# A unit's addition of sums tied behind a bank that VectorE empties, in a kernel of windowed attention and a gated feed-forward

## The chip, the cores and the metric

The kernel runs on one core of one Trainium2 chip. The metric is the device time of one execution in microseconds. Engines: TensorE (PE, with its weight loads PEld), VectorE (DVE), ScalarE (ACT), GpSimd (POOL) and SyncE (SP), which here issues nearly all transfers. Each engine takes its instructions in order.

## The reference

`x` has 2048 tokens of 512 values. It is normalised, goes through attention with 32 heads of 16 over a window of 256 tokens, and through a gated feed-forward of width 1792; the one output is gated by the other.

```
xn = layernorm(x)
q, k, v = split(xn @ wqkv)                        # 32 heads of 16
scores = where(0 <= i - j < 256, q k^T / 4, -1e9)
s = (softmax(scores) @ v) @ wo
h = silu(xn @ w1) * (xn @ w3)
out = x + s * silu(h @ w2)
```

## The kernel before

Products are made of float16 halves, a high and a low part, three matmuls for one. The tokens are cut into four tiles of 512 (`t`), the heads into four groups of eight (`g`); a tile and group are worked on in two **units** (`p`), each of four heads, 32 units in all. I count units from 0.

For a unit the kernel first finds the largest score of every row (`pass1`: scores by L619 into a PSUM bank, the maximum by L633 on VectorE), two units ahead, and then makes the scores again transposed (`pass2`: scores by L695, masks added by L702 on VectorE, the exponential by L705 on ScalarE) and multiplies them with the values (L723) into the PSUM tile `po`. There are two banks for scores (`s`); a bank is free when its maximum or its exponential has been taken. `po` has two halves, for the two halves of the keys, and a row of every head holds the sum of the exponentials.

When a unit's last chunk is multiplied, `finish` copies the first half to `os` on ScalarE (L733), and two steps later `rest` adds the second half on VectorE (L739). Then come the transfers: four of `os` into `on` (L745) and one of the sums into `dd` (L746). After the second unit of a tile and group `normalise` loads the sums as `dr` (L761); `invert` takes the reciprocal on VectorE (L765, L766), stores it as `de` (L768), spreads it by eight loads into `rb` (L772) and multiplies `on` by it on GpSimd (through `halves`, L307); `cut` makes the two float16 halves of the result (L778 on ScalarE, L307 on GpSimd), which the output projection reads (L996, `total`).

Attention alone would not fill TensorE. So each unit is run as five **batches** of scores (`batches`), and between them stands a share of dense work (`spread`): gate and up projections (`gate_up`, L897), the down projection (`down`, L946), the projections of q, k and v (L563, L533) and the output projection. A dense product goes into one of two PSUM banks `m0` and `m1` in turn (`bank`), and the bank must be emptied before TensorE comes to it again: on VectorE by L576 (q and k), L916 and L921 (gate and up), L967 and L970 (down) and L1000 (output), partly with an earlier copy on ScalarE (L572, L912).

Two things set the order. TensorE's instructions stand in the order in which the program makes them; those of the other engines are placed by a scheduler from their order in the program, their priority and its estimate of when their inputs are there. `urgent()` raises the priority. `tc.issue_after(ins)` makes the instructions in its block stand behind `ins` on the same engine, without a wait for a semaphore. And `later(n, f)` runs `f` after n more **steps**, where a step is one batch or one dense piece, some 18 of them in a unit; so it says how far on in the program the instructions of `f` are made.

Of the kernel before, what the change touches and what calls it, by code (L numbers as in the profile page):

```python
# [79 lines left out]
def tile_block(ctx: ExitStack, tc: tile.TileContext, x, wqkv, wo, w1, w3, w2, out):  # L80
# [466 lines left out]
    def project(t, g, k, terms=(range(3),), scores_bank=False):  # L547


        cell = {}  # L550

        parts = ([[(c, i) for c in (2 * half, 2 * half + 1) for i in range(3)] for half in range(2)] if len(terms) == 1
                 else [[(c, i) for i in group for c in range(NC)] for group in terms])

        def part(n):
            assert turned[t] == 4
            hi, lo, _ = WQK[g]
            xh, xl = X[t]
            if n == 0:
                cell["pp"] = pss.tile([P, 2, TW], F32, name="s")[:, 0, :] if scores_bank else bank([P, TW])  # L560
            for c, i in parts[n]:
                a, b = ((hi, xh), (lo, xh), (hi, xl))[i]
                nc.tensor.matmul(cell["pp"], a[:, k, c, :], b[:, c, :], start=(c, i) == parts[0][0],  # L563
                                 stop=(c, i) == parts[-1][-1])
            if n < len(parts) - 1:
                return
            pp = cell["pp"]
            both = take(F16)
            B = both.rearrange("p (a t) -> p a t", a=2)
            s = QS / (XS * WS)  # L570
            with urgent():
                nc.scalar.activation(B[:, 0, :], pp, AF.Copy, scale=s)  # L572

            def rest():
                with urgent():
                    nc.vector.scalar_tensor_tensor(B[:, 1, :], pp, s, B[:, 0, :], op0=ALU.mult, op1=ALU.subtract)  # L576
                d = (dQ, dK)[k][g][:, :, t * TW:(t + 1) * TW]
                if k == 0:
                    nc.sync.dma_start(d[:, 0:2, :], B[:, 0:1, :].to_broadcast([P, 2, TW]))
                    nc.sync.dma_start(d[:, 2, :], B[:, 1, :])  # L580
                else:
                    nc.sync.dma_start(d[:, 0:2, :], B)
                    nc.sync.dma_start(d[:, 2, :], B[:, 0, :])
                give(both, after=4)
            later(1, rest)
        return opening([(len(l), lambda n=n: part(n)) for n, l in enumerate(parts)])

# [86 lines left out]
    def pass2(t, g, p):  # L674

        es = WQK[g][2]
        cell = {}
        chunks = CHUNKS if t else FIRST

        def pieces(c):  # L680

            which, *halves, _ = chunks[c]
            for n in range(max(map(len, halves))):
                for a in which:
                    for h in range(2):
                        for piece in halves[h][n:n + 1]:
                            yield 256 * a * (len(which) - 1) + 64 * piece[3], h, a, piece

        def scores(c):
            qa, ka = QA[t, g], keys(t, g)  # L690
            s = scores_bank()
            for o, h, a, (m, k, n, _, _) in pieces(c):
                for r in range(2):
                    rows = slice(64 * r, 64 * r + KR + 2)
                    nc.tensor.matmul(s[64 * h:64 * h + 64, r, o:o + 64 * n], ka[rows, 2 * p + a, 64 * (m + 4):64 * (m + 5)],  # L695
                                     qa[rows, 2 * p + a, 64 * (m + k):64 * (m + k + n)], start=True, stop=True)
            which, *_, masks = chunks[c]
            sv = s.rearrange("p r (a k q) -> p (r a) k q", a=len(which), q=64)
            for first, by, n, kind, of in masks:
                v = sv[:, :, first:first + by * (n - 1) + 1:by, :]  # L700
                with urgent():
                    nc.vector.tensor_add(v, v, MK[:, kind, of:of + n, :].unsqueeze(1).to_broadcast([P, 2 * len(which), n, 64]))  # L702
            cell[c] = pt = ppool.tile([P, 2, 512], F32, name="pt")
            with urgent():
                nc.scalar.activation(pt, s, AF.Exp, scale=es)  # L705

        begun = set()

        def values(*cs):

            if not begun:
                cell["po"] = pso.tile([P, 2, TW], F32, name="po")
            turns = {}
            for c in cs:
                for item in pieces(c):
                    if item[3][4]:
                        turns.setdefault(item[1:3], []).append((c, *item))
            for group in zip_longest(*(turns[k] for k in sorted(turns))):
                for c, o, h, a, (m, k, n, _, _) in filter(None, group):
                    for r in range(2):  # L720
                        i = 2 * r + a
                        hd = g * 8 + r * 4 + 2 * p + a
                        nc.tensor.matmul(cell["po"][32 * i:32 * i + 32, h, 64 * (m + k):64 * (m + k + n)],  # L723
                                         V[64 * h:64 * h + 64, (4 * t + m // 2) % VB, hd * VW:hd * VW + 32],
                                         cell[c][64 * h:64 * h + 64, r, o:o + 64 * n],
                                         start=(h, i) not in begun, stop=c == len(chunks) - 1, skip_group_check=True)
                        begun.add((h, i))

        def finish():
            os = opool.tile([P, TW], F32, name="os", bufs=1)  # L730
            po = cell["po"]
            with urgent():
                nc.scalar.copy(os, po[:, 0, :])  # L733

            def rest():

                c = slice(0 if t else 64, TW)
                with urgent():
                    nc.vector.tensor_add(os[:, c], os[:, c], po[:, 1, c])  # L739
                if p == 0:  # L740
                    ON[t, g] = (opool.tile([P, TW], F32, name="on", bufs=1), dpool.tile([8, TW], F32, name="dd"))
                on, dd = ON[t, g]
                for i in range(4):
                    h = (i // 2) * 4 + 2 * p + i % 2
                    nc.sync.dma_start(on[16 * h:16 * h + 16, :], os[32 * i:32 * i + 16, :])  # L745
                nc.sync.dma_start(dd[4 * p:4 * p + 4, :], os[DH::32, :])  # L746
                if p == 1:
                    normalise(t, g)

            later(2, rest)  # L750

        def last(*cs):
            values(*cs)
            finish()
        n = len(chunks)
        return [lambda c=c: scores(c) for c in range(n)], lambda *cs: (last if cs[-1] == n - 1 else values)(*cs)

    def normalise(t, g):
# [16 lines left out]
        def cut():  # L775
# [1 line left out]
            O[t, g] = o = made.rearrange("p (a q) -> p a q", a=2)  # L777
            nc.scalar.copy(o[:, 0, :], on)  # L778
            halves(nc.gpsimd.tensor_sub, o[:, 1, :], on, o[:, 0, :])
        later(8, invert)  # L780
        later(24, cut)

# [101 lines left out]
    def gate_up(t, f):  # L886
        cell = {}

        def part(k, half):
# [18 lines left out]
            if k == 0:  # L908
                cell["s"] = sg = take(F32)

                with urgent():
                    nc.scalar.activation(sg, cell[0], AF.Tanh, scale=sg_scale[:, f:f + 1])  # L912

                def product():
                    with urgent():
                        nc.vector.scalar_tensor_tensor(sg, sg, 1.0, cell[0], op0=ALU.add, op1=ALU.mult)  # L916
                later(1, product)
            else:
                sg = cell["s"]
                with urgent():  # L920
                    nc.vector.scalar_tensor_tensor(sg, cell[1], 0.5 * HS / (WS * XS)**2, sg, op0=ALU.mult, op1=ALU.mult)  # L921
                HH[t, f] = hh = take(F16)

                def rest():
                    nc.scalar.copy(hh[:, 0:TW], sg)  # L925
                    halves(nc.gpsimd.tensor_sub, hh[:, TW:], sg, hh[:, 0:TW])
                    give(sg, after=4)
                later(1, rest)
# [5 lines left out]
    def down(t, k, b):  # L934
# [4 lines left out]
        def part(fs):  # L939
# [21 lines left out]
            if k == 0:  # L961
                ACC[t, b] = take(F32)
                with urgent():
                    if t:
                        nc.scalar.activation(ACC[t, b], ps, AF.Copy, scale=down_scale[:, 0:1])
                    else:
                        nc.vector.tensor_scalar(ACC[t, b], ps, down_scale[:, 0:1], None, op0=ALU.mult)  # L967
            else:
                with urgent():
                    nc.vector.scalar_tensor_tensor(ACC[t, b], ps, down_scale[:, k:k + 1], ACC[t, b], op0=ALU.mult, op1=ALU.add)  # L970
        return opening([(3 * len(fs), lambda fs=fs: part(fs)) for fs in (range(f0, f0 + 2), range(f0 + 2, f1))])

    def residual(t, b):
# [3 lines left out]
    def total(t, b):  # L977
# [4 lines left out]
        def part(half):  # L982
# [14 lines left out]
                                     stop=g == NG - 1 and i == 2)  # L997
            if half:
                with urgent():
                    nc.vector.scalar_tensor_tensor(y, ps, sc["y"], y, op0=ALU.mult, op1=ALU.mult)  # L1000
                if t == NT - 1:
                    nc.vector.tensor_add(y, y, XR[t, b])
                else:
# [326 lines left out]
```

## Time and profile before

| | |
|---|---|
| time, median of 3 runs | 830.6 us (830.26 to 831.95) |
| the profiled execution | 831.77 us, its span 830.0 us |
| TensorE busy | 806.0 us, 97% of the span |
| VectorE busy | 609.4 us, 73% |
| ScalarE, GpSimd busy | 406.0 us, 205.9 us |
| transfers | 110.65 MB, 133 GB/s on average |
| mean granted TensorE clock | 0.996 |

How to read it: a line of the profile that begins with a time is an instruction, or several equal ones in a row, on the engine's time line: start, duration, engine, source line, operation, what it writes and reads, shapes. In brackets behind it stands how long the engine was idle before it and whose end released it. In the list of waits, `DVE os L739 <- ACT os L733: 30.4, 24, 4.6` reads: VectorE stood 30.4 us before L739, in 24 waits of which the longest was 4.6 us, until L733 on ScalarE had ended.

### The profile page before, as it was taken

The page shows a single profiled execution, that of the slowest core. Times are in us where ns is not written, and L with a number is a line of the kernel's source. Part 1 is how long each engine was busy: PE and PEld are TensorE (multiplying, and loading weights), DVE is VectorE, ACT ScalarE, POOL GpSimd, SP SyncE. Part 2 cuts the span into 40 slices and gives each one's busy share as a digit, 9 for nine tenths or more (in the row PEclk, how much of TensorE's full clock was granted, in tenths as well). Part 3 has the DMA queues.
Part 4 walks back from the last instruction along what each step waited for, and adds up shares of the span by engine and source line. Part 5 has one row for each costly group of instructions (what it writes and reads, how often), then busy time and mean ns, then how long its engine had stood idle before and what let it go on. Part 6 is the DMA issues. An engine that isn't in the chain of part 4 may idle for free. (4 is left out here: it accounts for less than half of the span.)

```text
span 830.0 us, 22908 instructions
## 1 busy us (share of the span) xinstructions
PE 806.0 (97%) x8924; PEld 381.5 (46%) x8924; DVE 609.4 (73%) x1989; ACT 406.0 (49%) x594; POOL 205.9 (25%) x355
## 2 busy tenths in 40 slices
PE   8999889999999999999999999999999999999998
PEld 4434335544445444444444544444444444444444
DVE  8787687877697668778878777777677787676435
ACT  6889686644536444344343444443443444443521
POOL 2238174242213203121211211121111113030211
PEclk9999989999999999999999999999999999999999
DMA  9978556166533354544543444544545253343211
GB/s 282 268 231 236 183 158 208 58 172 196 151 104 101 98 146 124 158 119 135 145 108 88 103 112 133 135 110 117 136 105 142 80 140 95 102 127 89 66 20 53
DMA packets 95324, 110.65 MB, mean 133 GB/s; under 512 B 17200, under 2 KB 60528, under 8 KB 95216
## 3 DMA queue, kind: packets, MB, share of 16 engines
q1 hardware_dynamic: 94928, 108.67, 46.9%
q8 instruction: 70, 1.15, 0.6%
q10 hardware_dynamic: 288, 0.52, 0.2%
q14 instruction: 38, 0.31, 0.1%
HBM read 76.28 MB, written 28.57 MB: 126 GB/s over the span
## 5 line engine op out<-in xcount | busy, mean ns | idle before, releaser
L307 POOL TENSOR_TENSOR slot<-slot,slot 128x256 f16<-128x256 f32 (+1 forms) x228 | 151.4, 691 | 528.0 <-ACT slot L925 416.1
L897 PE MATMUL m<-XH,slot 128*128 128x512 f16 x896 | 268.2, 381 | 10.5 <-DVE slot L967 3.6
L705 ACT ACTIVATE pt<-s,es 128x1024 f32<-128x1024 f32 x152 | 167.5, 1113 | 171.6 <-DVE s L702 168.4
L897 PEld LDWEIGHTS <-slot 128*128 128x128 f16 x1344 | 125.2, 98 | 166.7 <-issue 23.0
L897 PE MATMUL m<-XL,slot 128*128 128x512 f16 x448 | 170.3, 380 | 0.0
L946 PE MATMUL m<-slot,slot 128*128 128x512 f16 x672 | 156.3, 380 | 1.1 <-DVE slot L576 0.7
L702 DVE TENSOR_TENSOR s<-s,MK 128x256 f32<-128x256 f32 (+2 forms) x280 | 118.4, 435 | 49.5 <-PE s L695 48.5
L633 DVE CUSTOM_DVE_ANT_0 junk<-s,MW 128x320 bf16<-128x320 f32 x276 | 134.3, 486 | 24.9 <-PE s L619 16.0
L946 PEld LDWEIGHTS <-slot 128*128 128x128 f16 x672 | 61.8, 98 | 79.2 <-issue 8.5
L633 DVE CUSTOM_DVE_ANT_0 junk<-po,MW 128x320 bf16<-128x320 f32 x172 | 83.6, 486 | 5.1 <-DVE al L279 0.4
L723 PE MATMUL po<-pt,V 64*32 64x320 f32 (+4 forms) x2880 | 77.2, 342 | 0.1
L925 ACT CAST slot<-slot 128x512 f16<-128x512 f32 x56 | 34.5, 616 | 69.9 <-DVE slot L921 69.6
L723 PEld LDWEIGHTS po<-pt,V 64*32 64x32 f32 x2880 | 51.1, 106 | 21.6 <-issue 0.8
L695 PE MATMUL s<-qa,KA 50*64 50x320 f16 (+3 forms) x1472 | 58.3, 260 | 0.7 <-ACT pt L705 0.7
L916 DVE SCALAR_TENSOR_TENSOR slot<-slot,m 128x512 f32<-128x512 f32 x56 | 38.3, 685 | 27.8 <-ACT slot L912 27.6
L695 PEld LDWEIGHTS <-KA 50*64 50x64 f16 x1472 | 30.4, 106 | 55.0 <-issue 37.0
L912 ACT ACTIVATE slot<-m,sgs 128x512 f32<-128x512 f32 x56 | 38.3, 684 | 30.7 <-PE m L897 30.4
L619 PE MATMUL s<-KA,qa 48*64 48x320 f16 (+3 forms) x824 | 45.6, 295 | 3.3 <-ACT pt L705 2.4
L921 DVE SCALAR_TENSOR_TENSOR slot<-m,slot 128x512 f32<-128x512 f32 x56 | 38.5, 687 | 12.0 <-PE m L897 11.4
L970 DVE SCALAR_TENSOR_TENSOR slot<-m,dsc,slot 128x512 f32<-128x512 f32 x48 | 35.9, 748 | 14.2 <-PE m L946 13.9
L563 PE MATMUL m<-XH,whi 128*128 128x512 f16 x120 | 45.2, 385 | 0.4 <-DVE slot L921 0.4
L739 DVE TENSOR_TENSOR os<-os,po 128x512 f32<-128x512 f32 (+1 forms) x32 | 21.5, 671 | 32.2 <-ACT os L733 30.4
(162 smaller groups left out, 892.7 us busy)
## 6 DMA issues: line engine op xcount, KB each, us to landing
slot<-dW SPq DMA_DIRECT2D x126, 256.0 KB
slot<-in_B_w_dram SPq DMA_DIRECT2D x42, 256.0 KB
dW<-slot SPq DMA_DIRECT2D x42, 256.0 KB
slot<-in_A_x_dram SPq DMA_DIRECT2D x30, 256.0 KB
KA<-dK SPq DMA_DIRECT2D x24, 288.0 KB
qa<-dQ SPq DMA_DIRECT2D x32, 192.0 KB
dQ<-slot SPq DMA_DIRECT2D x16, 256.0 KB
dK<-slot SPq DMA_DIRECT2D x16, 256.0 KB
```

Of the source, the lines that this page charges most:

```text
L307: op(out[:, c], a[:, c], b[:, c])
L563: nc.tensor.matmul(cell["pp"], a[:, k, c, :], b[:, c, :], start=(c, i) == parts[0][0], stop=(c, i) == parts[-1][-1])
L619: nc.tensor.matmul(s[c:c + w, r, :n], qa[rows, 2 * p + a, ii * P + c:ii * P + c + w], ka[rows, 2 * p + a, e - n:e], start=True, stop=True)
L633: lasts["maximum"] = nc.vector.tensor_tensor_reduce(out=junk[:, :n], in0=s[:, r, :n], in1=mask, scale=1.0, scalar=NEG, op0=ALU.add, op1=AL ...
L695: nc.tensor.matmul(s[64 * h:64 * h + 64, r, o:o + 64 * n], ka[rows, 2 * p + a, 64 * (m + 4):64 * (m + 5)], qa[rows, 2 * p + a, 64 * (m + k ...
L702: nc.vector.tensor_add(v, v, MK[:, kind, of:of + n, :].unsqueeze(1).to_broadcast([P, 2 * len(which), n, 64]))
L705: nc.scalar.activation(pt, s, AF.Exp, scale=es)
L723: nc.tensor.matmul(cell["po"][32 * i:32 * i + 32, h, 64 * (m + k):64 * (m + k + n)], V[64 * h:64 * h + 64, (4 * t + m // 2) % VB, hd * VW: ...
L897: nc.tensor.matmul(cell[k], w[:, (a * NC + c) * P:(a * NC + c + 1) * P], b[:, c, :], start=c == 0 and i == 0, stop=c == NC - 1 and i == 2)
L912: nc.scalar.activation(sg, cell[0], AF.Tanh, scale=sg_scale[:, f:f + 1])
L921: nc.vector.scalar_tensor_tensor(sg, cell[1], 0.5 * HS / (WS * XS)**2, sg, op0=ALU.mult, op1=ALU.mult)
L946: nc.tensor.matmul(ps, hh[:, a * TW + b * P:a * TW + (b + 1) * P], w[:, c * D:(c + 1) * D], start=f == f0 and i == 0, stop=f == f1 - 1 and ...
```

## The change

Each instruction with which VectorE empties a dense bank is noted in `lasts["emptied"]`, six places in all. The addition L739 is placed behind the last one noted, on VectorE. The transfers that follow it are a function of their own, `send`, run two steps after the addition. `invert` is due nine instead of eight steps after `normalise`, so three steps later in all; `cut` 22 instead of 24, so at the same step as before. No instruction is added or taken away.

```diff
             def rest():
 
                 c = slice(0 if t else 64, TW)
-                with urgent():
+
+                with urgent(), tc.issue_after(lasts["emptied"].ins):
                     nc.vector.tensor_add(os[:, c], os[:, c], po[:, 1, c])
+                later(2, send)
+
+            def send():
                 if p == 0:
                     ON[t, g] = (opool.tile([P, TW], F32, name="on", bufs=1), dpool.tile([8, TW], F32, name="dd"))
...
-        later(8, invert)
-        later(24, cut)
+        later(9, invert)
+        later(22, cut)
...
                 def product():
                     with urgent():
-                        nc.vector.scalar_tensor_tensor(sg, sg, 1.0, cell[0], op0=ALU.add, op1=ALU.mult)
+                        lasts["emptied"] = nc.vector.scalar_tensor_tensor(sg, sg, 1.0, cell[0], op0=ALU.add, op1=ALU.mult)
...
                 with urgent():
-                    nc.vector.scalar_tensor_tensor(ACC[t, b], ps, down_scale[:, k:k + 1], ACC[t, b], op0=ALU.mult, op1=ALU.add)
+                    lasts["emptied"] = nc.vector.scalar_tensor_tensor(ACC[t, b], ps, down_scale[:, k:k + 1], ACC[t, b],
+                                                                      op0=ALU.mult, op1=ALU.add)
```

The two shown are L916 and L970; L576, L921, L967 and L1000 are noted in the same form.

More of the change, by code (lines that the diff above doesn't have):

```diff
@@ L575, in rest @@
                 with urgent():
-                    nc.vector.scalar_tensor_tensor(B[:, 1, :], pp, s, B[:, 0, :], op0=ALU.mult, op1=ALU.subtract)
+                    lasts["emptied"] = nc.vector.scalar_tensor_tensor(B[:, 1, :], pp, s, B[:, 0, :], op0=ALU.mult, op1=ALU.subtract)
                 d = (dQ, dK)[k][g][:, :, t * TW:(t + 1) * TW]
@@ L920, in part @@
                 with urgent():
-                    nc.vector.scalar_tensor_tensor(sg, cell[1], 0.5 * HS / (WS * XS)**2, sg, op0=ALU.mult, op1=ALU.mult)
+                    lasts["emptied"] = nc.vector.scalar_tensor_tensor(sg, cell[1], 0.5 * HS / (WS * XS)**2, sg,
+                                                                      op0=ALU.mult, op1=ALU.mult)
                 HH[t, f] = hh = take(F16)
@@ L966, in part @@
                     else:
-                        nc.vector.tensor_scalar(ACC[t, b], ps, down_scale[:, 0:1], None, op0=ALU.mult)
+                        lasts["emptied"] = nc.vector.tensor_scalar(ACC[t, b], ps, down_scale[:, 0:1], None, op0=ALU.mult)
             else:
                 with urgent():
-                    nc.vector.scalar_tensor_tensor(ACC[t, b], ps, down_scale[:, k:k + 1], ACC[t, b], op0=ALU.mult, op1=ALU.add)
+                    lasts["emptied"] = nc.vector.scalar_tensor_tensor(ACC[t, b], ps, down_scale[:, k:k + 1], ACC[t, b],
+                                                                      op0=ALU.mult, op1=ALU.add)
         return opening([(3 * len(fs), lambda fs=fs: part(fs)) for fs in (range(f0, f0 + 2), range(f0 + 2, f1))])
@@ L999, in part @@
                 with urgent():
-                    nc.vector.scalar_tensor_tensor(y, ps, sc["y"], y, op0=ALU.mult, op1=ALU.mult)
+                    lasts["emptied"] = nc.vector.scalar_tensor_tensor(y, ps, sc["y"], y, op0=ALU.mult, op1=ALU.mult)
                 if t == NT - 1:
```

## The prediction

> **What bounds the kernel now.** I read the page first, for the engine that is never free, then the stretches of the run, then the waits, and last the engines' own time lines at the places where TensorE stands still.
>
> ```profile
> PE 806.0 (97%) x8924; PEld 381.5 (46%) x8924; DVE 609.4 (73%) x1989; ACT 406.0 (49%) x594; POOL 205.9 (25%) x355
> ```
>
> ```profile
> 0.00:230.00 230.00, 213.54 (x2013) 99.67 (x2013) 176.46 (x663) 155.72 (x282) 88.05 (x173) 0.99 0.66 193
> 230.00:830.00 600.00, 592.50 (x6912) 281.80 (x6911) 432.98 (x1327) 250.29 (x312) 117.81 (x182) 1.00 0.41 110
> ```
>
> The first line says TensorE bounds the run: 806.0 of 830.0 us. The second fence (a stretch, its length, busy time of PE, PEld, DVE, ACT, POOL, then the granted clock) says where the rest lies: 16.5 us of idle in the first 230 us, and 7.5 us in the 600 us after, some of it the drain at the end. So a change to VectorE's order has something to win only in the first seven or eight units, and something to lose everywhere.
>
> ```profile
> DVE os L739 <- ACT os L733: 30.4, 24, 4.6
> PE m L897 <- DVE slot L967: 3.6, 1, 3.6
> PE m L897 <- DVE slot L921: 3.0, 1, 3.0
> PE s L619 <- ACT pt L705: 2.4, 5, 0.7
> ```
>
> In the waits (total, times, longest) VectorE stands 30.4 us in front of the addition L739, for ScalarE's copy of the other half. Whatever is behind the addition stands too. TensorE pays for it at two places: 3.6 us for the bank that L967 empties and 3.0 us for the one of L921. In the built program these two are exactly the instructions right behind the addition. Of the 32 additions 16 are moved behind one such emptying (units 0 to 3, 8 to 12, 19, 21, 23 to 26 and 29, counted from 0); the other 16 keep their place, being behind theirs already. TensorE's own order is the same. So the change does what it says, in half of the units, and 6.6 us of visible waits hang on it.
>
> **Unit 0: the wait changes hands.**
>
> ```profile
> 84.54 1.47 PE L946 MATMUL m<-slot,slot 128*128 128x512 f16 x6
> 86.34 2.76 PE L946 MATMUL m<-slot,slot 128*128 128x512 f16 x12
> 92.71 0.59 PE L897 MATMUL m<-XH,slot 128*128 128x512 f16 x2 [3.61 <-DVE slot L967]
> 94.10 0.41 PE L695 MATMUL s<-qa,KA 50*64 50x320 f16 x10
> 94.67 0.25 PE L619 MATMUL s<-KA,qa 48*64 48x128 f16 x4 [0.16 <-ACT pt L705]
> ...
> 86.66 0.17 DVE L859 CAST sb<-ssq 128x4 bf16<-128x4 f32 x1 [0.30 <-ACT sqa L855]
> 91.38 0.62 DVE L739 TENSOR_TENSOR os<-os,po 128x448 f32<-128x448 f32 x1 [4.55 <-ACT os L733]
> 91.92 0.74 DVE L967 TENSOR_SCALAR slot<-m,dsc 128x512 f32<-128x512 f32 x1
> 92.57 0.42 DVE L702 TENSOR_TENSOR s<-s,MK 128x256 f32<-128x256 f32 x1
> ...
> 90.78 0.56 ACT L733 COPY os<-po 128x512 f32<-128x512 f32 x1
> 93.50 1.11 ACT L705 ACTIVATE pt<-s,es 128x1024 f32<-128x1024 f32 x1 [1.54 <-DVE s L702]
> ```
>
> The bank of L967 is full at 84.54 + 1.47 = 86.0, VectorE is free at 86.8, so ahead of the addition L967 ends near 87.6, before TensorE comes for the bank at 86.34 + 2.76 = 89.1. The 3.61 us are gone. But the addition still cannot start before the copy ends (90.78 + 0.56 = 91.3), and behind it on VectorE are the masks L702, on ScalarE behind those the exponential L705, and TensorE's scores L619 wait for L705's bank (the 0.16 at 94.67). The masks come sooner only by what L967 took between the two, 92.57 - 91.92 = 0.65. TensorE does its piece of L897 (94.10 - 92.71 = 1.39 us) from 89.1 to 90.5 and then stands before the scores, L695 and L619, until about 94.02 instead of 94.67. Gain: 0.65 us, not 3.6; late next is L702, held by the same copy.
>
> **Unit 1.**
>
> ```profile
> 114.46 0.65 DVE L873 TENSOR_SCALAR sw<-p,q 128x4 f32<-128x4 f32 x1
> 115.46 0.62 DVE L739 TENSOR_TENSOR os<-os,po 128x448 f32<-128x448 f32 x1 [0.35 <-ACT os L733]
> 117.14 0.29 DVE L702 TENSOR_TENSOR s<-s,MK 128x128 f32<-128x128 f32 x1
> ...
> 118.11 1.11 ACT L705 ACTIVATE pt<-s,es 128x1024 f32<-128x1024 f32 x1
> 119.12 0.71 ACT L310 ACTIVATE slot<-slot,sw 128x512 f32<-128x512 f32 x1
> ...
> 116.73 0.59 PE L897 MATMUL m<-XH,slot 128*128 128x512 f16 x2 [3.00 <-DVE slot L921]
> 119.27 0.32 PE L619 MATMUL s<-KA,qa 48*64 48x128 f16 x4 [0.51 <-ACT pt L705]
> ```
>
> L921 moves up to 114.46 + 0.65 = 115.1 and ends at 115.8, so TensorE restarts 0.9 us before 116.73, but meets L619 at 119.27 again: L705 started at 118.11 though its mask was there at 117.43, because ScalarE was busy with the weights' cuts (its row for 114.67 to 118.08, below, has no idle). In the built program one more of these, L310, stands ahead of L705. That costs 0.71 less the 0.10 by which the two overlap (118.11 + 1.11 - 119.12), 0.61 us. With the 0.65 of unit 0 carried along, the sum at 119.3 is -0.04.
>
> **Units 2 and 3.**
>
> ```profile
> 146.26 0.41 PE L695 MATMUL s<-qa,KA 50*64 50x320 f16 x9 [0.18 <-ACT pt L705]
> 169.35 0.25 PE L619 MATMUL s<-KA,qa 48*64 48x128 f16 x4 [0.74 <-ACT pt L705]
> ...
> 168.19 1.11 ACT L705 ACTIVATE pt<-s,es 128x1024 f32<-128x1024 f32 x1
> 169.20 0.61 ACT L311 CAST slot<-slot 128x512 f16<-128x512 f32 x1
> ```
>
> In unit 2 the masks come sooner and TensorE's 0.18 us go. In unit 3 a cast, L311, is put ahead of L705 in the same way: 0.61 less the same overlap, +0.51. Sum: -0.04 - 0.18 + 0.51 = +0.29 us.
>
> **The later units.**
>
> ```profile
> 345.29 0.69 DVE L739 TENSOR_TENSOR os<-os,po 128x512 f32<-128x512 f32 x1 [0.44 <-ACT os L733]
> 346.08 0.75 DVE L970 SCALAR_TENSOR_TENSOR slot<-m,dsc,slot 128x512 f32<-128x512 f32 x1
> 346.74 0.69 DVE L702 TENSOR_TENSOR s<-s,MK 128x512 f32<-128x512 f32 x1
> 347.53 1.11 ACT L705 ACTIVATE pt<-s,es 128x1024 f32<-128x1024 f32 x1 [2.27 <-DVE s L702]
> ```
>
> Here the addition filled the time in which L970 waited for TensorE to fill its bank. Moved behind, it leaves VectorE standing at L970 with the addition and the masks queued behind it, and the masks come later by the addition less the overlap, 0.6 us. I take nothing for it, from the row of the second stretch: TensorE has 592.50 of 600 us there, it queues scores two banks ahead, and L705 itself stood idle for 2.27 us without TensorE's feeling it. Six units look like this one; uncovered they would cost 3.6 us. The PSUM tile po, which the addition frees, is wanted again two batches later.
>
> **Transfers and inversion.** The transfers L745 and L746, and for every second unit dr (L761), are emitted two steps later, the inversion three; the cut stays where it was. On SP's queue dr falls behind dm (L656) in several tiles, and de and rb behind the loads of qa.
>
> ```profile
> 172.76 0.38 SPq L761 DMA_DIRECT2D dr<-dd  x1
> 173.24 0.38 SPq L656 DMA_DIRECT2D dm<-mt  x1
> ...
> DVE dr L765 <- DMA dr<-dd: 11.9, 9, 4.1
> POOL on L307 <- DMA rb<-de: 36.5, 5, 14.2
> ```
>
> One place is 0.48 us. The reciprocal L765 keeps its place on VectorE in most tiles, so VectorE stands that much longer for dr there, and the masks and banks behind it too. The bounds are nine waits at 0.48, +4.3 us, and a small gain where L765 itself is moved back. I take 0, near the waits of TensorE: 11.9 us of VectorE's standing here left none there under its name. GpSimd's product waits longer for rb, the cut behind it too; the output projection reads it a tile or more later, which hides it, and uncovered it is again 0.48 for each load that rb falls behind. At the end of the run no engine's order changes.
>
> **The clock.**
>
> ```profile
> 90.77:94.18 3.41, 1.47 (x10) 0.57 (x13) 2.80 (x10) 1.87 (x6) 0.00 (x0) 1.00 0.26 82
> 114.67:118.08 3.41, 1.34 (x6) 0.48 (x5) 3.06 (x10) 3.41 (x8) 1.24 (x3) 1.00 0.96 305
> 118.08:124.91 6.83, 6.32 (x34) 2.58 (x34) 4.27 (x16) 6.83 (x14) 5.95 (x10) 0.50 0.46 143
> ```
>
> After unit 1's stall the granted clock is 0.50 for 6.83 us; from 119.27 on that costs half of 5.64, 2.8 us. The half-length stretch before it had TensorE busy for 1.34 us; the one at unit 0 had 1.47 and was followed by full clock. After the change unit 1 has two stands of about 2 us (113.1 to 115.2, and to 119.2) with the same 2.0 us of work between them (116.73 to 118.76 before), busier than 1.34, so this stretch may go: -2.8. Unit 0 in 90.77 to 94.18 has only the 0.41 of L695 and 0.16 of L619 left, so one may come there: +1.7 (half of 3.41) to +3.4 (half of 6.83), of which unit 1's stand takes back some 0.5. Both together give -1.6 to +0.1; I take -0.8.
>
> By the Trainium skill, "TensorE: Matmul & The Clock Gate", Part 1, the array drops to half clock after at least one idle window of about 3.4 us and returns after a busy one, the windows running freely. The trace agrees on the length and differs on the idleness: 1.34 us of work did not save the clock. Taken by the word, no half-clock stretch would be left, which is the first rival.
>
> **Sum.** +0.3 - 0.8 = -0.5. The profiled execution took 831.77 us beside its span of 830.0, 1.2 above the median of 830.6; it becomes 831.3, and the median 830.1 us. 0.2% (1.7 us) is about what a measurement here can tell from no change, so this is no change.
>
> **Rivals.**
> - The half clock goes and no new one comes: 830.6 + 0.3 - 2.8 = 828.1. For it: the 2.1 us waits. Against: the rows at unit 0.
> - Both waits go whole: 830.6 - 6.6 = 824.0. For it: the waits. Against: the masks L702 hang on the same copy.
> - Slower: the longer stand at unit 0 brings a half clock there and the one at 118 stays. It decides once TensorE's work in such a stretch falls under about 1.4 us. Price 1.7 to 3.4, middle 2.5 less 0.5 hidden: 830.6 + 0.3 + 2.0 = 832.9.
> - Slower by the reciprocal: dr late in most tiles, half of the 4.3 us reaching TensorE: 830.6 + 0.3 + 2.1 = 833.0. For it: L765 has VectorE's longest waits for a transfer. Against: TensorE's list.
>
> **Chances.** No change 0.42 (own range 828.9 to 832.2); half clock gone 0.24; both waits 0.06; new half clock 0.20; reciprocal 0.08. Faster 0.24 + 0.06 = 0.30, slower 0.28. The range from 827.6 to 832.9 leaves out the 824 case, and the upper half of the slower two: 0.06 + 0.14.
>
> **What would show it.** TensorE's wait for L967 at 89 gone, and one of two to three us before L695 or L619 at 91 to 94 in its place; VectorE's wait before L739 still over 25 us in total; the granted clock in 90 to 125. The forecast is wrong if the masks of unit 0 come before 91.3, if the idle in the first 230 us falls by over 3 us, or if the later 600 us lose over 1 us of TensorE's work.

## The result, and the profile after

| | before | after |
|---|---|---|
| median | 830.49 us (829.81 to 831.95, 8 runs) | 834.71 us (833.11 to 835.92, 8 runs) |
| ratio, 95% interval | | 1.0046 (1.0034 to 1.0059) |
| profiled execution, its span | 831.77, 830.0 us | 835.89, 834.0 us |
| mean granted clock | 0.996 | 0.993 |

The change makes the kernel 4.2 us slower. The forecast was 830.1, range 827.6 to 832.9: wrong. In the changed kernel lines from L739 on carry other numbers: the addition is L740, the emptyings L916, L921 and L967 are L920, L925 and L972, the reciprocal is L769, `de` L772, `rb` L776, ScalarE's cut L782, and the matmuls L897, L946 and L996 are L901, L951 and L1002.

The page's busy time of the engines, and two stretches of the changed kernel (length, busy time and number of instructions of PE, PEld, DVE, ACT and POOL, granted clock, share and GB/s of the transfers). In all fences of this text, rows that stand between those shown are left out.

```profile
PE 807.7 (97%) x8924; PEld 381.5 (46%) x8924; DVE 609.7 (73%) x1989; ACT 406.1 (49%) x594; POOL 205.8 (25%) x355
```

```profile
0.00:230.00 230.00, 214.12 (x2021) 99.74 (x2025) 176.64 (x664) 156.14 (x283) 88.06 (x173) 0.99 0.65 194
230.00:834.00 604.00, 593.54 (x6911) 281.77 (x6903) 433.04 (x1326) 249.98 (x312) 117.72 (x182) 1.00 0.39 109
```

In the first 230 us TensorE's idle time is a little less, 15.9 for 16.5 us. Behind it the idle time has grown from 7.5 to 10.5 us. The loss is not where the waits were that the change aimed at. The changed kernel's waits over the whole run (total, times, longest):

```profile
POOL on L307 <- DMA rb<-de: 46.5, 8, 13.7
...
ACT slot L782 <- POOL on L307: 29.7, 11, 8.1
...
DVE os L740 <- ACT os L733: 22.3, 10, 5.4
...
PE s L619 <- ACT pt L705: 5.4, 4, 2.3
PE m L901 <- DVE slot L920: 5.1, 3, 3.0
...
PE s L695 <- DVE M L633: 2.0, 1, 2.0
```

TensorE's 3.6 us before the bank of L967 are gone. A new wait of 3.0 us stands before a bank of L920. ScalarE's longest wait for GpSimd's product `on` times `rb`, ahead of its cut, has grown to 8.1 us; before, its row was this:

```profile
ACT slot L778 <- POOL on L307: 27.8, 11, 4.3
```

Since TensorE's order is the same in both kernels, each of its instructions can be set against itself. Just ahead of the new wait the changed kernel was 1.4 us in front; at 555.21 in the kernel before it is 1.7 us behind, a few matmuls later 3.0. Of the 1.4 us it had 0.8 already at 528 us. That is not to be put down to the change: run 3 below, whose order is the old one up to there, was 1.2 us in front at that place. First the kernel before, then the changed one, on TensorE's time line:

```profile
555.21 0.59 PE L897 MATMUL m<-XH,slot 128*128 128x512 f16 x2
...
556.60 0.41 PE L695 MATMUL s<-qa,KA 50*64 50x320 f16 x8
```

```profile
556.92 1.01 PE L901 MATMUL m<-XH,slot 128*128 128x512 f16 x2 [3.00 <-DVE slot L920]
...
559.57 0.60 PE L695 MATMUL s<-qa,KA 50*64 50x320 f16 x8
```

The stand is 3.0 us, and 1.25 more (559.57 - 556.60, less 556.92 - 555.21) go in a stretch at half clock behind it (1.01 us for the two matmuls that took 0.59). From 540 us, where the changed kernel is 0.8 us in front, to 560, where it is 3.2 behind, it loses 4.0 us. That is the loss. What stands behind it is seen on the other engines. The kernel before, units 19 and 20:

```profile
529.57 0.69 DVE L739 TENSOR_TENSOR os<-os,po 128x512 f32<-128x512 f32 x1 [0.22 <-DMA KA<-dK]
538.72 0.34 DVE L765 RECIPROCAL dr<-dr 128x32 f32<-128x32 f32 x1
...
539.36 0.32 SPq L768 DMA_DIRECT2D de<-dr  x1
541.12 5.15 SPq L772 DMA_DIRECT2D rb<-de  x8
...
549.00 1.42 POOL L307 TENSOR_TENSOR on<-on,rb 128x256 f32<-128x256 f32 x2
...
550.45 0.62 ACT L778 CAST slot<-on 128x512 f16<-128x512 f32 x1 [3.66 <-POOL on L307]
550.98 0.58 ACT L733 COPY os<-po 128x512 f32<-128x512 f32 x1
...
551.59 0.69 DVE L739 TENSOR_TENSOR os<-os,po 128x512 f32<-128x512 f32 x1 [0.57 <-ACT os L733]
```

The changed kernel:

```profile
529.53 0.75 DVE L1006 SCALAR_TENSOR_TENSOR slot<-m,us,slot 128x512 f32<-128x512 f32 x1 [1.01 <-PE m L1002]
530.20 0.68 DVE L740 TENSOR_TENSOR os<-os,po 128x512 f32<-128x512 f32 x1
540.72 0.35 DVE L769 RECIPROCAL dr<-dr 128x32 f32<-128x32 f32 x1
...
539.86 0.81 SPq L595 DMA_DIRECT2D qa<-dQ  x2
541.63 0.34 SPq L772 DMA_DIRECT2D de<-dr  x1
542.08 0.36 SPq L801 DMA_DIRECT2D slot<-dW  x1
545.42 3.80 SPq L776 DMA_DIRECT2D rb<-de  x8
...
552.41 1.41 POOL L307 TENSOR_TENSOR on<-on,rb 128x256 f32<-128x256 f32 x2 [4.82 <-DMA rb<-de]
...
553.85 0.62 ACT L782 CAST slot<-on 128x512 f16<-128x512 f32 x1 [8.13 <-POOL on L307]
554.38 0.58 ACT L733 COPY os<-po 128x512 f32<-128x512 f32 x1
...
554.99 0.69 DVE L740 TENSOR_TENSOR os<-os,po 128x512 f32<-128x512 f32 x1 [5.42 <-ACT os L733]
555.59 0.69 DVE L702 TENSOR_TENSOR s<-s,MK 128x512 f32<-128x512 f32 x1
556.19 0.68 DVE L920 SCALAR_TENSOR_TENSOR slot<-slot,m 128x512 f32<-128x512 f32 x1
```

Read it downward. The addition of unit 19 waits behind an emptying whose bank is not full yet (1.01 us). The reciprocal stands behind work that it preceded before (the scheduler, it seems, expects `dr` later): 10.5 us behind the addition, not 9.2. SyncE issues both loads of `qa` from `dQ` ahead of `de`, where before `de` came first. The trace records when each transfer has landed: `de` took 3.8 us from its issue (landed at 545.41, and `rb` is issued at 545.42), where it took 1.4 before. GpSimd multiplies 3.4 us later. ScalarE has the cut of that product in its queue ahead of the next unit's copy of sums, and stands 8.1 us before it. Behind the copy are the addition, the masks and the emptying L920 on VectorE, and TensorE's bank is behind that.

The Trainium skill says in "TensorE: Matmul & The Clock Gate", Part 1, "Architectural detail", that ScalarE and VectorE take their instructions strictly first in, first out. The trace agrees: the copy of sums starts 0.53 us after the cut in both kernels, whenever the cut starts, and in run 5 below, where it is put ahead of the cut, it starts 4.5 us before it.

### The profile page after: what moved, and what is told of

Its sections match the earlier page's. It is cut to its first block, busy times and chain, and to the rows that moved or that the text cites. A ratio compares the mean times of both kernels' runs of the same rounds, so it can differ in the third digit from the quotient of the medians.

```text
span 834.0 us, 22899 instructions
## 1 busy us (share of the span) xinstructions
PE 807.7 (97%) x8924; PEld 381.5 (46%) x8924; DVE 609.7 (73%) x1989; ACT 406.1 (49%) x594; POOL 205.8 (25%) x355
## 5 line engine op out<-in xcount | busy, mean ns | idle before, releaser
L901 PE MATMUL m<-XH,slot 128*128 128x512 f16 x896 | 269.9, 383 | 8.8 <-DVE slot L920 5.1
L901 PEld LDWEIGHTS <-slot 128*128 128x128 f16 x1344 | 125.7, 98 | 166.3 <-issue 21.6
L901 PE MATMUL m<-XL,slot 128*128 128x512 f16 x448 | 171.3, 382 | 0.0
L951 PE MATMUL m<-slot,slot 128*128 128x512 f16 x672 | 156.5, 380 | 1.6 <-DVE slot L576 0.7
L951 PEld LDWEIGHTS <-slot 128*128 128x128 f16 x672 | 61.8, 98 | 80.0 <-issue 9.5
L920 DVE SCALAR_TENSOR_TENSOR slot<-slot,m 128x512 f32<-128x512 f32 x56 | 38.4, 685 | 28.1 <-ACT slot L916 27.8
L916 ACT ACTIVATE slot<-m,sgs 128x512 f32<-128x512 f32 x56 | 38.3, 684 | 28.2 <-PE m L901 27.8
L619 PE MATMUL s<-KA,qa 48*64 48x320 f16 (+3 forms) x824 | 45.4, 294 | 6.8 <-ACT pt L705 5.4
L925 DVE SCALAR_TENSOR_TENSOR slot<-m,slot 128x512 f32<-128x512 f32 x56 | 38.5, 688 | 13.7 <-PE m L901 13.2
L563 PE MATMUL m<-XL,whi 128*128 128x512 f16 x120 | 45.0, 383 | 0.0
```

Source lines behind the costliest of these rows:

```text
L619: nc.tensor.matmul(s[c:c + w, r, :n], qa[rows, 2 * p + a, ii * P + c:ii * P + c + w], ka[rows, 2 * p + a, e - n:e], start=True, stop=True)
L901: nc.tensor.matmul(cell[k], w[:, (a * NC + c) * P:(a * NC + c + 1) * P], b[:, c, :], start=c == 0 and i == 0, stop=c == NC - 1 and i == 2)
L920: lasts["emptied"] = nc.vector.scalar_tensor_tensor(sg, sg, 1.0, cell[0], op0=ALU.add, op1=ALU.mult)
L925: lasts["emptied"] = nc.vector.scalar_tensor_tensor(sg, cell[1], 0.5 * HS / (WS * XS)**2, sg, op0=ALU.mult, op1=ALU.mult)
L951: nc.tensor.matmul(ps, hh[:, a * TW + b * P:a * TW + (b + 1) * P], w[:, c * D:(c + 1) * D], start=f == f0 and i == 0, stop=f == f1 - 1 and ...
```

## The experiments

Theory (the **chain theory** of the expectations): one tied addition, unit 19's, causes the loss by this chain. Rivals: the later step counts of `send`, `invert` and `cut`; a little from each of the sixteen moved additions; a way from the late transfers to TensorE that does not go by ScalarE's queue. Each run is compared with the kernel before on the same chip, whose medians were 830.53 us for the first four, 831.27 for the next four and 831.41 for the last; so it is the ratios that compare.

**1. The tie alone**, on the changed kernel.

```diff
-                later(2, send)
+                send()
...
-        later(9, invert)
-        later(22, cut)
+        later(8, invert)
+        later(24, cut)
```

> The tie alone; sends, inversion and cut at the step counts of the kernel before. Chain theory (the stall of 3.00 us at 553.93 and the half clock behind it, 4.4 us together, come from the tied addition of the unit that ends at 530: its sums, the reciprocal and the spread of rb land later, ScalarE's cut of the output tile waits for them and stands ahead of the next copy of sums): that stall stays, and only the 1.0 us at 774, whose order on VectorE is the old one here, comes back: 833.7 us, 833.0 to 834.3. Steps theory (the later step counts cost, the tie costs nothing): no stall over 1 us between 540 and 780, 829.1 to 830.5 us. Spread theory (all sixteen moved additions cost a little each): 832 to 833.5 with no single stall over 1 us behind 200 us.

Measured: 834.89 us, ratio 1.0036 (1.0017 to 1.0055). The stall is there, 2.71 us before L901 at 557.79, with half clock behind it. By the ratio 3.0 us are lost; the median is above the 833.0 to 834.3 us expected. The tie does it.

**2. The step counts alone**, on the changed kernel.

```diff
-                with urgent(), tc.issue_after(lasts["emptied"].ins):
+                with urgent():
```

> No tie; the sends 2 steps later, the inversion 9 steps behind them, the cut 22. Chain theory: VectorE's order differs in one place only (one pair at 367) and ScalarE's in one, so the time stays within 0.6 us of the kernel before, 829.9 to 831.1, the wait of 3.61 us at 90 stays as it was, and TensorE has no stall over 1.5 us between 540 and 780. Steps theory: 833.5 to 835 us with the stall at 554. Spread theory: as the chain theory, 830.5.

Measured: 830.97 us, ratio 1.0008 (0.9995 to 1.002), no stall over 0.8 us behind 200 us. The later steps cost nothing that can be measured, and they hardly move an instruction: on VectorE one pair changes places, at 367 us. Presumably the scheduler goes by when it expects the inputs; that was not tested.

**3. The tie in unit 19 alone**, on the kernel before, and **4. everything but that tie**, on the changed kernel.

```diff
-                with urgent():
-                    nc.vector.tensor_add(os[:, c], os[:, c], po[:, 1, c])
+                def add():
+                    nc.vector.tensor_add(os[:, c], os[:, c], po[:, 1, c])
+                with urgent():
+                    if (t, g, p) == (2, 1, 1):     # run 4: != in place of ==
+                        with tc.issue_after(lasts["emptied"].ins):
+                            add()
+                    else:
+                        add()
```

> The kernel before with the tie in one unit alone, the one whose addition VectorE does at 529.57. By the order of the instructions, on VectorE the addition goes behind one emptying and the reciprocal with its product two operations back (538.72 to about 541); ScalarE's and GpSimd's orders are the old ones. Chain theory: this alone brings the stall of 2.5 to 3.0 us at 552 to 554 and perhaps the half clock: 833 to 835 us, with TensorE's shift zero until 540. Steps theory and spread theory: 830.2 to 830.9 us, no stall over 1 us there.

> The changed kernel without the tie in that same unit, all else as changed. Chain theory: the stall at 554 goes, and with it its half clock: 834.7 less 4.4 and, with the 1.0 us at 774 left, 830.3 us, 829.5 to 831. Steps theory and spread theory: 834.3 to 834.8 us, the stall at 554 still there.

Measured: the one tie gives 834.24 us, ratio 1.0044 (1.0029 to 1.0059), all of the change's loss; the changed kernel without it gives 831.16 (0.2 over the range expected), ratio 1.0004 (0.9993 to 1.0015). One of 32 ties is the cause, and the spread theory and the steps theory fall.

The times of run 3 lie far apart, 830.3 to 836.7 us, and the execution that was profiled is its quickest. That shows the chain from the other side (from `de` on, its line numbers are six above those of the changed kernel):

```profile
529.85 0.68 DVE L740 TENSOR_TENSOR os<-os,po 128x512 f32<-128x512 f32 x1
...
541.28 0.34 SPq L778 DMA_DIRECT2D de<-dr  x1
541.73 0.37 SPq L807 DMA_DIRECT2D slot<-dW  x1
543.75 3.79 SPq L782 DMA_DIRECT2D rb<-de  x8
...
549.24 1.41 POOL L307 TENSOR_TENSOR on<-on,rb 128x256 f32<-128x256 f32 x2 [1.99 <-DMA rb<-de]
...
550.68 0.62 ACT L788 CAST slot<-on 128x512 f16<-128x512 f32 x1 [5.31 <-POOL on L307]
...
553.76 0.59 PE L907 MATMUL m<-XH,slot 128*128 128x512 f16 x2 [0.18 <-DVE slot L926]
```

The order around unit 19 is the same as in the changed kernel, but here the product starts 7.96 us behind the issue of `de`, there 10.78 us. The 2.8 us by which the transfers were quicker are the 2.8 us by which TensorE's stand is shorter, 0.18 for 3.00. Run 1, with the same order there, fits in: 10.49 us, and a stand of 2.71. So the late order alone eats up the slack, and the landing of the transfers decides whether TensorE pays.

**5. The cut behind the copy of sums**, on the changed kernel, and **6. the same on the kernel before.**

```diff
-                nc.scalar.copy(os, po[:, 0, :])
+                lasts["os"] = nc.scalar.copy(os, po[:, 0, :])
...
-            nc.scalar.copy(o[:, 0, :], on)
+            with tc.issue_after(lasts["os"].ins):
+                nc.scalar.copy(o[:, 0, :], on)
```

> The changed kernel with ScalarE's cut of the output tile put behind the copy of the next unit's sums in ScalarE's order (13 of its 32 places swap; VectorE's, GpSimd's and TensorE's orders stay). The reciprocal, the transfers and GpSimd's product stay as late as in the changed kernel. Chain theory (what reaches TensorE is the wait of 8.13 us in which ScalarE stands before the cut, with the copy of sums behind it): the stall at 554 shrinks below 0.7 us and its half clock goes, 834.7 less 4.4 is 830.3 us, 829.6 to 831.3. Rival (the late transfers reach TensorE in another way, through the one buffer of the output tile or of the sums): a stall of 2 us or more stays between 545 and 580, 833 to 835 us.

> The same edit on the kernel before (sixteen cuts go behind the copy of sums). Chain theory: no cut holds a copy there for longer than VectorE's slack, so 829.9 to 831.0 us, no difference. Rival: the waits of 27.8 us before the cut cost something in many units, 828.5 to 829.8 us.

Measured: run 5 gives 832.57 us, ratio 1.0015 (1.0001 to 1.003): about a third of the loss is left. Run 6 gives 830.64, ratio 0.9991 (0.998 to 1.0002), no difference. Run 5 falls between the two expectations, and its trace says why (the cut, the tanh, the emptying and the matmul are one line further down here, L783, L917, L921 and L902):

```profile
549.24 0.59 ACT L733 COPY os<-po 128x512 f32<-128x512 f32 x1 [3.66 <-PE po L723]
553.72 0.62 ACT L783 CAST slot<-on 128x512 f16<-128x512 f32 x1 [3.89 <-POOL on L307]
554.24 0.68 ACT L917 ACTIVATE slot<-m,sgs 128x512 f32<-128x512 f32 x1
...
555.69 0.59 PE L902 MATMUL m<-XH,slot 128*128 128x512 f16 x2 [1.91 <-DVE slot L921]
```

The copy is free, but the next in ScalarE's queue is the tanh of the gate, and TensorE's bank hangs on that as well. A stand of 1.91 us is left, without half clock.

**9. The cut behind the latest exponential**, on the changed kernel.

```diff
-                nc.scalar.activation(pt, s, AF.Exp, scale=es)
+                lasts["pt"] = nc.scalar.activation(pt, s, AF.Exp, scale=es)
...
-            nc.scalar.copy(o[:, 0, :], on)
+            with tc.issue_after(lasts["pt"].ins):
+                nc.scalar.copy(o[:, 0, :], on)
```

> The changed kernel with ScalarE's cut behind the latest exponential instead (at the stall of 554 it goes behind the copy of sums, the tanh and the exponential; TensorE's and VectorE's orders do not move). The run before this one, with the cut behind the copy of sums alone, kept a stall of 1.91 us, put down to the tanh of the hidden tile, which is then the next instruction behind the cut. Chain theory: the stall at 554 is under 0.7 us, and the loss of 4.4 us is gone: 829.8 to 831.2 us. Rival (a late output tile reaches TensorE by another way, its one buffer or the transfers of the sums): a stall over 1 us remains between 545 and 580, 832 to 834.5 us.

Measured: 830.37 us, ratio 0.9984 (0.9971 to 0.9997), all its times under 831.8. With all sixteen ties in place and `rb` as late as ever in the order, the loss is gone. What reached TensorE went through ScalarE's queue, and the one buffer of `on` plays no part that can be measured. The profiled execution had quick transfers (product at 549.34), so it cannot show a late cut being harmless; the eleven times do. None of them is 833 us or more, where nine of run 1's twelve and eight of run 3's twelve are. (Of the kernel before, 5 of 35 are on this chip.)

**7. The tie in unit 0 alone** and **11. in units 0 to 3**, on the kernel before: the edit of run 3 with `(t, g, p) == (0, 0, 0)` and with `t == 0 and g < 2`.

> The kernel before with the tie in the first unit alone: one swap on VectorE (the addition of 91.38 goes behind the emptying of 91.92), nothing else moves on any engine. By the prediction's first step TensorE stands again at 94.02 in place of 94.67: 0.65 us less, 829.8 us, if the half clock at 118 stays; up to 2.8 less, 827.7, if it goes; 1.7 more if one more stretch at half clock follows the first wait. Rival: no gain, 830.5, since the wait changes its place only.

> The kernel before with the tie in the first four units alone (times of the first 200 us tell; all later additions stay). The prediction's steps for these units add up to +0.1 us (-0.65, +0.61, -0.18, +0.29) and its clock term to -0.8: 829.8 us, and 830.6 if the stretch at half clock stays as long. Rival (the loss lies in these units after all, by the exponentials that wait behind two cuts of ScalarE): 832 us or more. TensorE's shift at 224 us should be between -0.9 and +0.3.

Measured: 830.29 us, ratio 0.9989 (0.9978 to 1.0001), and 829.81 us, ratio 0.9986 (0.9972 to 1.0). Both have the sign of the prediction's steps, at the edge of what can be told from nothing; the rival of run 11, 832 us or more, falls. In run 11's trace TensorE is at 224 us where it is in the kernel before, a shift of 0.0 where -0.9 to +0.3 was expected, and it has a stretch at half clock at 94.8 us, of which more below.

**8, 10 and 12: versions that may beat both.** Unit 0's tie with the cut behind the copy of sums (8) or behind the exponential (10), and the ties of units 0 and 2 with the latter (12).

> Both: the tie in the first unit alone, and every cut behind the copy of sums. Sum of the two: 829.8 us by the chain theory, between 828 and 830.5; it is the version that may beat both kernels. Rival: the swaps in the order of the sums' transfers cost, over 831.

> The kernel before with the tie in the first unit alone and the cut behind the latest exponential. Chain theory: as with the cut behind the copy of sums, 828.5 to 830 us, 0.1 to 0.25% under the kernel before on the same chip. Rival: cuts that come 3 to 7 places later on ScalarE delay GpSimd's cut and the output projection, over 831 us.

> The kernel before with the tie in the first and the third unit and the cut behind the latest exponential. By the prediction's third step the third unit gains 0.18 us: 0.1 to 0.3 us under the version with the first unit's tie alone, which five rounds cannot tell from no difference; 828.3 to 830 us. Rival: the third unit's mask, which goes ahead of the addition, brings nothing, and the later sums cost as they do in the unit at 530: over 831 us.

Measured: 829.44 us, ratio 0.9979 (0.9968 to 0.9989); 830.49 us, 0.9986 (0.997 to 1.0001); 830.3 us, 0.998 (0.9961 to 0.9999). Run 8 beats both kernels, by 1.7 us and, going by the two ratios, by 5.6; the three are not told apart from each other. The medians of runs 10 and 12 are 0.5 and 0.3 us over the ranges expected.

## Why the prediction was wrong, by its steps

**Unit 0** was right. The wait changed hands as worked out: 3.61 us before L967's bank became 2.00 and 0.59 us before the scores, and the scores came at 93.80, where 94.02 was forecast. That it came out so near is in part luck: in this execution TensorE was 0.39 us behind at 84 us, so it gained 1.26 and not 0.65. The other 0.61 is the copy's, behind which the addition started at 91.16 for 91.38. TensorE's and VectorE's time lines of the changed kernel:

```profile
92.79 0.41 PE L695 MATMUL s<-qa,KA 50*64 50x320 f16 x10 [2.00 <-DVE M L633]
93.80 0.25 PE L619 MATMUL s<-KA,qa 48*64 48x128 f16 x4 [0.59 <-ACT pt L705]
...
91.16 0.62 DVE L740 TENSOR_TENSOR os<-os,po 128x448 f32<-128x448 f32 x1 [3.29 <-ACT os L733]
```

**Units 1 to 3** were right: TensorE stands 2.02 us before L925's bank and then 2.29 before L619 for the exponential behind ScalarE's cuts, and in unit 3 it stands 1.80 us where it stood 0.74. Set against itself, TensorE loses 0.67 us from 100 to 119.3 us (0.61 forecast) and 0.52 in unit 3 (0.51 forecast). At 223.8 the changed kernel was 0.24 us in front; the steps with the clock term had said 0.5.

**The later units** were right about the masks, wrong about one of them. The additions behind banks that are not full cost TensorE nothing that can be measured (run 4 keeps all but one of them); unit 19's cost it through what is behind the addition, the transfers. VectorE's waits for the copy before the addition were expected to stay over 25 us in all; they fell to 22.3.

**Transfers and inversion** is the step that failed. It took 0 and bounded it by VectorE's nine waits for `dr`, which are ten now and as long in all (12.0 us for 11.9). Where the reciprocal moves back on VectorE it expected "a small gain". That is unit 19 above all, and the gain was there: TensorE's wait of 0.42 us before 543.73 for VectorE's maxima is gone, and it comes 0.6 us further in front, as in all five profiled kernels with this tie and in no other. What the late reciprocal cost behind it was left out. The prediction let the late `rb` be hidden because "the output projection reads it a tile or more later". It looked at who reads the cut's result. It did not look at what is queued behind the cut on ScalarE: a copy of sums on which VectorE and, 2.5 us later, a bank of TensorE hang. The row of ScalarE's 27.8 us before L778 stood in the list of waits, and the prediction does not use it. The rival of the reciprocal has the right start, a late `dr`, and the wrong way. Measured, the term is 4.0 us: the stand of 3.0, some 1.5 at half clock, less the gain of 0.6.

**The clock.** Taken at -0.8; the stretches at half clock in the changed kernel (granted clock 0.50), all 3.41 us long, two of them with the stretch ahead of them:

```profile
116.28:119.69 3.41, 1.09 (x23) 0.70 (x23) 1.36 (x5) 3.41 (x7) 3.27 (x5) 1.00 0.60 203
119.69:123.10 3.41, 3.41 (x10) 1.19 (x9) 3.17 (x13) 3.16 (x6) 3.37 (x6) 0.50 0.75 223
...
170.89:174.30 3.41, 3.41 (x9) 1.22 (x8) 3.12 (x14) 1.60 (x2) 0.59 (x1) 0.50 0.57 173
553.19:556.60 3.41, 0.74 (x4) 0.22 (x3) 1.61 (x3) 1.91 (x4) 1.93 (x3) 1.00 0.05 20
556.60:560.01 3.41, 3.09 (x18) 1.05 (x21) 1.87 (x6) 1.38 (x2) 0.00 (x0) 0.50 0.22 53
```

The one of 6.83 us behind unit 1 became 3.41, which is a gain, and a new one behind unit 3's stand took it back. No new one came at unit 0, so the rival of 832.9 us, a half clock there, did not occur in this execution. But it can: of the ten profiled kernels that tie unit 0, six (runs 1, 5, 9, 10, 11, 12) have a stretch at half clock of 3.4 or 6.8 us that begins at 92.6 to 96.3 us, and four have none. Of the four that do not tie it, runs 3 and 6 have one too, at 93.5 and 92.1 us. So the stretches of one execution are weak ground for a clock term of -0.8.

**What stays open.** The delay from addition to cut is 23.65 us in the changed kernel and 20.88 before; of the difference the order on VectorE has 1.4 us, and the transfers with their place in SyncE's order most of the rest (the landing of `de` alone 2.3 us, of which GpSimd hides some: before, it multiplied 1.3 us after `rb` was there). These two were not undone one by one. In the changed kernel's profile TensorE also stands 1.46 us near 774, where the reciprocal again stands behind an emptying that it preceded before, waits 1.79 us for `dr`, and holds up the masks. Run 4, with the same order there, has 0.90 us of that wait, and TensorE loses 0.2.

Why the same transfers land 2.8 us sooner in some executions was not tested, but the traces point to a cause. A transfer's landing is recorded in sixteen parts. In the changed kernel fifteen parts of `de` are there by 544.05 and the last at 545.41; of the last `rb`, fifteen by 550.61 and the last at 552.11. These two late parts, 1.4 and 1.5 us, come to about the 2.8. During both, a transfer of instructions of 16 KB was under way (on the queue that the page calls instruction, 542.93 to 544.33 and 549.30 to 550.73). Run 1 is alike. In run 3 the second transfer of instructions starts at 549.36, after `rb` was there (548.95), and the last part of `de` is 0.3 us late. No run moved these transfers, so the cause is argued and not shown.

## What to carry to other kernels

When something is made later, ask of each instruction that waits for it what stands behind that instruction on its engine, and not only who reads its result: here a float16 cut that nobody needed for tens of microseconds (the output projection of its tile waits for unit 23 too, whose sums are added at 621.8) held TensorE up. A tie in a scheduled kernel moves everything that the scheduler times by the tied instruction; compare the whole orders, and tie only where the trace shows a wait. A filler instruction that waits for a transfer belongs behind the urgent ones of its engine, which alone undid the loss here.

## What the runs showed of the hardware

As the traces count it, the half clock does not go by TensorE's busy time in the stretch before alone. The stretch 112.87 to 116.28 of the changed kernel, with TensorE busy for 1.40 us, was followed by full clock, and 167.48 to 170.89, with 1.60 us, by half:

```profile
112.87:116.28 3.41, 1.40 (x6) 0.48 (x5) 3.27 (x14) 2.87 (x7) 1.33 (x3) 1.00 0.85 273
...
167.48:170.89 3.41, 1.60 (x25) 0.85 (x18) 0.81 (x2) 2.57 (x4) 3.41 (x7) 1.00 0.73 238
```

The first holds 6 records of large matmuls, the second 25 mostly small ones. Runs 6 and 11 agree: 1.56 us in 14 records (115.97 to 119.38) was followed by full clock, 1.63 us in 25 (91.34 to 94.75) by half. What is counted stays open. And one transfer chain of the same order took 7.96 us in one execution and 10.78 in another, so where the slack behind it is smaller than the difference, the time of the kernel depends on the landing, as in run 3.
